# Token transfers over 128 partitions in one DMA, ScalarE copies ahead of some products, and a new order, in an S4 + gated-MLP block

## The chip, the cores and the metric

One core of one Trainium2 chip. The time is device microseconds (us) of one execution, the median over several. With one core a run's state can only be told from other runs of the same kernel: a run over 1.5% above the fastest is called slow.

## The reference, cut to what matters

```python
# L = 2048 tokens, D = 512 channels, F = 1792 hidden, N = 128 modes; bfloat16
x  = A_u                                   # [1, 2048, 512]
xn = layernorm(x)
def _A_ref(u, A, B, C, log_dt, Dskip):     # S4: a long convolution per channel
    K  = einsum("dn,dnl,dn->dl", C, exp(dt * A * l), dt * B).real
    y  = irfft(rfft(pad(u)) * rfft(pad(K)))[:L]
    return y + u * Dskip
def _B_ref(x, w_gate, w_up, w_down):       # gated MLP
    h = sigmoid(x @ w_gate) * (x @ w_up)
    return h @ w_down
return x + _A_ref(xn, ...) + _B_ref(xn, ...)
```

## The kernel before

Every operation is recorded with its engine, its inputs and the buffers that it takes and frees, and then emitted in a fixed list `ORDER`. The engines run their own streams in that order and wait for each other through semaphores. The parts that the change touches:

```python
# token t = (2*a + j)*16 + i sits in partition 64*j + a
xv   = A_u[0].rearrange("(a j i) d -> j a i d", j=2, i=NT)
outv = out[0].rearrange("(a j i) d -> j a i d", j=2, i=NT)

def load_x(i0, n):                         # first token loads: i0 = 0, 2, 4, 8, 12
    ls = [load("ACT" if i0 < 4 and j else "SP", xn[64 * j:64 * j + 64, i0:i0 + n, :],
               xv[j][:, i0:i0 + n, :], 64 * n * KB, pkt=1024 * n, hv=1 - j) for j in range(2)]
# ... (cut)
le = dma("SP", es, cten["E"].ap()[:, gs, :, :], ...)(320 * KB)   # one unit of the spectrum table
# ... (cut)
def final(t, gdeps):                       # output of 2 token rows per partition
    # ... (cut: inverse transform on TensorE, add on VectorE into one of 3 output buffers)
    a = dma("SP", outv[0][:, isl, :], lambda: ot()[0:64], deps=[fin], ...)(128 * KB)
    dma("ACT", outv[1][:, isl, :], lambda: ot()[64:128], deps=[fin, a], rel=[osl], ...)(128 * KB)
# ... (cut)  gated MLP, 4 token groups x 14 units:
mu = pl.add("PE", 0.864, fu, ...)          # up product into a PSUM bank (one of 3)
def fpd(sl=b, h=h):                        # sigmoid(gate) * up, up read from PSUM
    V.tensor_tensor(out=h(), in0=h(), in1=bank(sl), op=ALU.mult)
prods.append(pl.add("DVE", 0.60, fpd, [es_, mu], PPROD, rel=[b]))
# ... (cut)  last group: residual rows of its tokens, 512 KB
lx = [dma("SP", xt[64 * j:64 * j + 64], xv[j][:, i:i + 4, :], ...)(256 * KB) for j in range(2)]
# ... (cut)  other groups: residual added into the MLP's result by the DMA itself
for j in range(2):
    def facc(i=i, j=j, fx=fx):
        P.dma_start(out=fx()[64 * j:64 * j + 64], in_=xv[j][:, i - 1:i + 1, :], accum_op=ALU.add)
final(i // 2, acc)
```

PE is TensorE, DVE VectorE, ACT ScalarE, POOL GpSimd (it issues the accumulating DMAs on a software queue), SP SyncE (it issues most other DMAs). SBUF is the on-chip memory, laid out in 128 partitions; PSUM is the one that TensorE writes its results to, in banks.

## Time and profile before

| | before |
|---|---|
| median of four runs | 275.37 us (274.05 to 276.51) |
| span of the profiled run, granted clock | 276.0 us, 0.965 |
| VectorE busy, TensorE busy | 208.6 us (76%), 229.2 us (83%) |
| last up product (TensorE's) ends | 251.36 us |
| from there to the end | 24.6 us |

The span in 40 slices of 6.9 us (the page's part 2). Each digit is a slice's busy share in tenths; `PEclk` is the clock granted to TensorE, in tenths of full speed; the last row is what the DMA engines moved. VectorE stands at 8 or 9 from slice 4 to slice 20, and nearly so to slice 28, so it bounds that stretch; TensorE follows. The last slices move 134 and 97 GB/s.

```profile
PE   7299997969969899878598878596998689799792
...
DVE  3579899998999999999979997979153222685172
...
PEclk9779999997999999999999999989999979999998
...
GB/s 152 190 297 306 201 307 77 40 57 76 31 190 160 233 160 128 100 183 28 184 185 143 222 159 46 130 153 125 93 221 178 223 199 112 190 187 181 217 134 97
```

The chain of waits that ended last (part 4), shares of the span by engine:

```profile
PE 40%; DVE 29%; DMA 16%; ACT 6%; issue 4%; SPq 2%; DVEq 0%; ACTq 0%
```

VectorE's groups by form: the product (L964 of the kernel file), and a multiply of the same size with both inputs in SBUF. Columns: busy us, mean ns of one | idle time before, with what ended it. Reading one input from PSUM makes the same arithmetic take 682 in place of 421 ns.

```profile
L964 DVE TENSOR_TENSOR hT_sb<-hT_sb,bank 128x512 bf16<-128x512 bf16 x56 | 37.0, 682 | 10.7 <-PE bank L957 6.0 <-ACT hT_sb L951 3.7 <-ACT ln_m_f L467 0.8
...
L680 DVE TENSOR_TENSOR big<-big 128x512 bf16<-128x512 bf16 x8 | 3.4, 421 | 0.0
```

The token transfers among the DMA issues: number, KB of each, median us from issue to landing. `POOLq` rows are the accumulations.

```profile
big<-in_A_u_dram SPq DMA_DIRECT2D x8, 256.0 KB, 7.2
glu_sb<-in_A_u_dram POOLq DMA_DIRECT2D x8, 128.0 KB, 3.9
...
out_dram<-big SPq DMA_DIRECT2D x7, 128.0 KB, 3.0
```

Moments of the timeline (start us, length, engine, what, idle time before in brackets): first tokens in, first gate matmul, first up matmul, first product, first output store, and the last eight that SyncE issues. The whole lead-in to the first product is 29 us.

```profile
4.13 0.69 DVE L499 BATCH_NORM_STATS2 stats<-big 128x6 f32<-128x512 bf16 x1 [4.13 <-DMA big<-in_A_u_dram]
...
15.17 12.71 PE L942 MATMUL bank<-xnT,wg_sb 128*128 128x256 bf16 x64
27.72 4.48 PE L957 MATMUL bank<-xnT,wu_sb 128*128 128x512 bf16 x20
...
28.85 0.69 DVE L964 TENSOR_TENSOR hT_sb<-hT_sb,bank 128x512 bf16<-128x512 bf16 x1 [0.75 <-ACT ln_m_f L467]
...
254.84 0.55 SPq L397 DMA_DIRECT2D out_dram<-big  x1
...
263.01 9.67 SPq L397 DMA_DIRECT2D out_dram<-big  x8
```

### The profile page before, as it was taken

How to read it: one execution, taken by the hardware profiler on the slowest of the kernel's cores; microseconds unless marked ns; L12 is line 12 of the kernel's file. 1: busy time of each engine (PE TensorE's matmuls, PEld its weight loads, DVE VectorE, ACT ScalarE, POOL GpSimd, SP SyncE). 2: the span in 40 equal slices, each digit the busy share in tenths (PEclk: the TensorE clock that was granted, in tenths of full speed). 3: DMA queues.
4: the chain of work that ended last, by engine and by line, in shares of the span. 5: the costliest groups of instructions: out<-in, count | busy, mean ns of one | idle time of the engine just before them, and what ended most of it. 6: DMA issues, size and time to landing. Idle time of an engine off the chain costs nothing.

```text
span 276.0 us, 5805 instructions
## 1 busy us (share of the span) xinstructions
PE 229.2 (83%) x2290; PEld 117.6 (43%) x2290; DVE 208.6 (76%) x407; ACT 162.7 (59%) x249; POOL 20.8 (8%) x43
## 2 busy tenths in 40 slices
PE   7299997969969899878598878596998689799792
PEld 2264433323323544355354445243665345444441
DVE  3579899998999999999979997979153222685172
ACT  2289999998998572558385549341356758531000
POOL 3225000020020002003000000000011200000000
PEclk9779999997999999999999999989999979999998
DMA  5899992122066764451765751454386984665743
GB/s 152 190 297 306 201 307 77 40 57 76 31 190 160 233 160 128 100 183 28 184 185 143 222 159 46 130 153 125 93 221 178 223 199 112 190 187 181 217 134 97
DMA packets 51069, 43.42 MB, mean 157 GB/s; under 512 B 13153, under 2 KB 44258, under 8 KB 51042
## 3 DMA queue, kind: packets, MB, share of 16 engines
q1 hardware_dynamic: 47506, 38.73, 50.1%
q0 software_dynamic: 960, 1.57, 3.9%
q10 hardware_dynamic: 2576, 2.75, 3.5%
q8 instruction: 18, 0.29, 0.5%
q14 instruction: 9, 0.07, 0.1%
HBM read 24.43 MB, written 12.06 MB: 132 GB/s over the span
## 4 chain that ended last, share of the span: by engine, by line
PE 40%; DVE 29%; DMA 16%; ACT 6%; issue 4%; SPq 2%; DVEq 0%; ACTq 0%
PE bank L942 11%; PE bank L957 9%; DMA big<-z_scr 8%; PE bank L982 6%; DVE big L681 5%; DVE big L680 5%; PE pair L744 4%; DVE hT_sb L964 4%; PE pair L835 4%; DVE big L685 4%; DVE big L686 3%; DMA ident<-c_ident 3%; DMA big<-big 2%; DMA big<-v_scr 2%; SPq L397 2%
## 5 line engine op out<-in xcount | busy, mean ns | idle before, releaser
L942 PE MATMUL bank<-xnT,wg_sb 128*128 128x512 bf16 (+1 forms) x236 | 57.4, 382 | 1.4 <-ACT hT_sb L951 1.4
L957 PE MATMUL bank<-xnT,wu_sb 128*128 128x512 bf16 x224 | 55.9, 384 | 2.9 <-ACT hT_sb L951 1.5
L982 PE MATMUL bank<-wd_sb,hT_sb 128*128 128x512 bf16 x224 | 52.2, 387 | 3.3 <-ACT glu_sb L1012 3.3
L964 DVE TENSOR_TENSOR hT_sb<-hT_sb,bank 128x512 bf16<-128x512 bf16 x56 | 37.0, 682 | 10.7 <-PE bank L957 6.0
L951 ACT ACTIVATE hT_sb<-bank 128x512 bf16<-128x512 f32 x56 | 32.3, 599 | 15.1 <-PE bank L942 15.0
L841 DVE TENSOR_TENSOR big<-big 128x2048 bf16<-128x2048 bf16 x16 | 19.6, 1223 | 24.8 <-DMA big<-big 8.2
L680 DVE TENSOR_TENSOR big<-big 128x256 bf16<-128x256 bf16 (+5 forms) x52 | 33.1, 636 | 2.5 <-ACT big L721 1.4
L942 PEld LDWEIGHTS <-wg_sb 128*128 128x128 bf16 x236 | 22.8, 101 | 27.9 <-issue 6.8
L982 PEld LDWEIGHTS <-hT_sb 128*128 128x128 bf16 x224 | 21.7, 99 | 30.4 <-issue 6.9
L681 DVE TENSOR_TENSOR big<-big 128x256 bf16<-128x256 bf16 (+5 forms) x52 | 32.9, 633 | 0.0
L957 PEld LDWEIGHTS <-wu_sb 128*128 128x128 bf16 x224 | 20.5, 98 | 28.5 <-issue 7.7
L822 ACT ACTIVATE big<-pair 128x1024 bf16<-128x1024 f32 x16 | 16.3, 1026 | 11.4 <-PE pair L817 7.3
L685 DVE TENSOR_TENSOR big<-big 128x128 bf16<-128x128 bf16 (+5 forms) x52 | 21.9, 420 | 0.8
L835 PE MATMUL pair<-big 128*128 128x256 bf16 x160 | 20.4, 278 | 2.2 <-ACT big L837 0.7
L862 ACT ACTIVATE big<-pair 128x1024 bf16<-128x1024 f32 x16 | 16.4, 1026 | 9.0 <-PE pair L858 5.2
L686 DVE TENSOR_TENSOR big<-big 128x128 bf16<-128x128 bf16 (+5 forms) x52 | 21.6, 416 | 0.0
L837 ACT ACTIVATE big<-pair 128x1024 bf16<-128x1024 f32 x16 | 16.4, 1027 | 7.8 <-PE pair L835 3.4
L835 PEld LDWEIGHTS <-big 128*128 128x128 bf16 x160 | 15.9, 100 | 8.2 <-issue 3.0
L744 PE MATMUL pair<-big 128*32 128x82 bf16 x512 | 11.5, 257 | 8.2 <-DVE big L685 6.3
L645 ACT ACTIVATE big<-pair 128x1024 bf16<-128x1024 f32 x16 | 16.3, 1019 | 1.7 <-DMA z_scr<-big 1.0
L858 PE MATMUL pair<-big 64*64 64x256 bf16 x384 | 13.7, 272 | 3.1 <-ACT big L822 1.6
L817 PE MATMUL pair<-big,m 64*64 64x256 bf16 x128 | 6.6, 288 | 10.2 <-DMA big<-z_scr 10.2
(84 smaller groups left out, 234.2 us busy)
## 6 DMA issues: line engine op xcount, KB each, us to landing
big<-c_E SPq DMA_DIRECT2D x16, 320.0 KB, 4.2
z_scr<-big SPq DMA_DIRECT2D x16, 256.0 KB, 2.6
big<-z_scr SPq DMA_DIRECT2D x16, 256.0 KB, 4.6
big<-big SPq DMA_DIRECT2D x64, 64.0 KB, 2.9
v_scr<-big SPq DMA_DIRECT2D x16, 256.0 KB, 2.6
big<-v_scr SPq DMA_DIRECT2D x12, 256.0 KB, 4.6
big<-in_A_u_dram SPq DMA_DIRECT2D x8, 256.0 KB, 7.2
wu_sb<-in_B_w_up_dram SPq DMA_DIRECT2D x2, 896.0 KB, 6.1
```

Source lines behind the costliest of these rows:

```text
L680: V.tensor_tensor(out=wide(outp), in0=lov, in1=mre, op=ALU.mult)
L681: V.tensor_tensor(out=wide(tb()), in0=lov, in1=mim, op=ALU.mult)
L685: V.tensor_tensor(out=outp[:, :, :, 0, :], in0=outp[:, :, :, 0, :], in1=tb()[:, :, :, 1, :], op=opr)
L686: V.tensor_tensor(out=outp[:, :, :, 1, :], in0=outp[:, :, :, 1, :], in1=tb()[:, :, :, 0, :], op=opi)
L744: T.matmul(pk[32 * t:32 * t + 32, y % 4, :], G[:, r, :, comp, h], H[:, r, :, comp, h], start=(comp == 0), stop=(comp == 1), tile_position= ...
L835: T.matmul(two(sk)[:, o:o + DW], es()[:, g, kt, :], kT[p][:, kt, :], start=kt in (0, NKT - 1), stop=kt >= NKT - 2)
L841: V.tensor_tensor(out=pp().rearrange("p q h m -> p (q h) m"), in0=xx().rearrange("p q h m -> p (q h) m"), in1=kb()[:, 0:2 * DW].unsqueeze( ...
L942: T.matmul(bank(sl)[:, c0:c1], w[:, kt, k * 128:(k + 1) * 128], xnT[:, grp, kt, c0:c1], start=(kt == 0), stop=(kt == KT - 1))
L951: S.activation(out=hT_sb[:, hs.idx, k % 2, :], in_=bank(sl), func=ACT.Sigmoid)
L957: T.matmul(bank(sl), wu_sb[:, kt, k * 128:(k + 1) * 128], xnT[:, grp, kt, :], start=(kt == 0), stop=(kt == KT - 1))
L964: V.tensor_tensor(out=h(), in0=h(), in1=bank(sl), op=ALU.mult)
L982: T.matmul(bank(po), hT_sb[:, hts[k // 2].idx, k % 2, jj * 128:(jj + 1) * 128], wd_sb[:, k, :], start=(k == 0), stop=k == FT - 1, **kw)
```

## The change

Its intent: fewer DMA issues, by moving all 128 partitions of a token transfer at once; a spectrum unit that lies contiguous in memory; cheaper products, by letting ScalarE copy 27 of the 56 up products out of PSUM as bf16 first (which also frees the PSUM bank earlier); and an order made for this. Costs such as 0.55 in `pl.add` only serve to find an order; the device sees `ORDER` alone.

```diff
-                ... E=f(_build_E(S1, M2)))
+                ... E=f(_build_E(S1, M2).reshape(128, NU // 2, 2, NKT, 128).transpose(1, 0, 2, 3, 4)))
+UEV = (1, 8, 13, 14, 16, 18, 19, 24, 25, 26, 28, 29, ..., 42, 45, 48)      # 27 units
-ORDER = [1, 29, 0, 3, 2, 39, ...]                                          # cut
+ORDER = [1, 43, 0, 3, 4, 12, ...]                                          # cut

 def load_x(i0, n):
-    ls = [load("ACT" if i0 < 4 and j else "SP", xn[64 * j:64 * j + 64, i0:i0 + n, :], xv[j][:, i0:i0 + n, :], 64 * n * KB,
-               pkt=1024 * n, hv=1 - j) for j in range(2)]
+    ls = [load("ACT" if i0 == 2 else "SP", xn[:, i0:i0 + n, :], xv[:, :, i0:i0 + n, :].rearrange("j a i d -> j a (i d)"), 128 * n * KB,
+               pkt=1024 * n)]
...
-            le = dma("SP", es, cten["E"].ap()[:, gs, :, :], deps=w_use[0], ...)(320 * KB)
+            le = dma("SP", es, cten["E"].ap()[u], deps=w_use[0], ...)(320 * KB)
...
-        a = dma("SP", outv[0][:, isl, :], lambda: ot()[0:64], deps=[fin], ...)(128 * KB)
-        dma("ACT", outv[1][:, isl, :], lambda: ot()[64:128], deps=[fin, a], rel=[osl], ...)(128 * KB)
+        dma("SP", outv[:, :, isl, :].rearrange("j a i d -> j a (i d)"), lambda: ot(), deps=[fin], rel=[osl], ...)(256 * KB)
...
-                def fpd(sl=b, h=h):
-                    V.tensor_tensor(out=h(), in0=h(), in1=bank(sl), op=ALU.mult)
-                prods.append(pl.add("DVE", 0.60, fpd, [es_, mu], PPROD, rel=[b]))
+                def feu(sl=b, us=us, on=on):
+                    if on:
+                        S.activation(out=us_sb[:, us.idx, :], in_=bank(sl), func=ACT.Identity)
+                eu = pl.add("ACT", 0.48, feu, [mu], PSIG, acq=[us] if on else [], rel=[b] if on else [], alt=(un, 1))
+                def fpd(sl=b, h=h, us=us, on=on):
+                    V.tensor_tensor(out=h(), in0=h(), in1=us_sb[:, us.idx, :] if on else bank(sl), op=ALU.mult)
+                prods.append(pl.add("DVE", 0.33, fpd, [es_, eu, mu], PPROD, rel=[us] if on else [b], alt=(un, 2)))
...
-                    lx = [dma("SP", xt[64 * j:64 * j + 64], xv[j][:, i:i + 4, :], ...)(256 * KB) for j in range(2)]
+                    lx = [dma("SP", xt, xv[:, :, i:i + 4, :].rearrange("j a i d -> j a (i d)"), ...)(512 * KB)]
...
-                for j in range(2):
-                    ...  P.dma_start(out=fx()[64 * j:64 * j + 64], in_=xv[j][:, i - 1:i + 1, :], accum_op=ALU.add)
+                    ...  P.dma_start(out=fx(), in_=xv[:, :, i - 1:i + 1, :].rearrange("j a i d -> j a (i d)"), accum_op=ALU.add)
```

The stores of the last group are merged in the same way (cut). A merged 256 KB transfer then has, in elements (step, count), the DRAM side `[8192, 2] [16384, 64] [1, 1024]` and the SBUF side `[59392, 128] [1, 1] [1, 1024]`. The 2 at the front of the DRAM side is `j`.

## The prediction

> **What bounds it now.** From about 30 to 165 us VectorE is saturated (97 to 99% busy in the table of windows; 208.6 us in all); TensorE, 83% busy over the span, is the nearest limit afterwards. The chain of waits is mostly TensorE (40%) and VectorE (29%), DMA 16%. The timeline shows a short start: first tokens landing 3.4 us after their issue, first gate matmul at 15.2, first up matmul at 27.7, first product at 28.9 us. The tail is short: 128 KB stores land in a median 2.5 to 3.0 us (page, DMA issues).
>
> **Gains.** 27 of 56 products read a bf16 SBUF copy in place of PSUM: 682 ns now; the 128x512 bf16 SBUF multiplies of line 680 take 421 ns (groups by form). That is 27 x 0.26 = 7 us off VectorE, for 27 x 0.6 = 16 us more on ScalarE, which is 59% busy. Most lie in groups 1 and 2, in or near the VectorE-bound stage: worth about 5 us. Spectrum rows keep their 2,560 bytes (320 KB, 4.2 us to landing): under 1 us. Fewer issues (185 to 179 on SyncE, about 0.6 us each) remove little, since SyncE mostly waits.
>
> **Costs.** A 128-row token transfer has the DRAM side [2][64][row] against [128][row] in SBUF. The Trainium skill, "DMA: Bandwidth & Descriptors", section "Why a DMA increments its semaphore by 16 and not by 1", says a DMA is split over the largest k up to 16 that divides the slowest dimension of both sides. Here that is 2. The trace of before agrees where it can be tested: SyncE's queue shows 3,089 four-byte completion packets, 1 modulo 16, and one transfer has one row; 64-row transfers show 16 each. So token transfers go from 16 DMA engines to 2. A 2,048-byte packet takes 84 ns, so 64 packets per engine take 5.4 us for 256 KB; 512 KB about 10.6 us. Whatever is issued behind them waits for its share on those two engines.
>
> Start: the first two loads share the two engines and land near 13 us in place of 4. The next two (512 KB each) stand in front of the later gate weights, B, and the up weights: gate weights near 40 us, up weights 46 to 49, first product about 50. Both bounding engines fall some 20 to 25 us behind; product saving and slack return part: +15 us at the tail.
>
> Tail: the output is 2 MB, 7 stores of 256 KB and smaller ones, about 44 us on two engines, all behind down projection 13; three output buffers come free only as stores land. Estimated from the last up product to the end: 55 us in place of 25, so +30.
>
> **Sum:** 276 + 15 + 30 = about 320 us; range 288 to 348. Faster by over 2%: 0.13; within 2%: 0.06; slower: 0.81.
>
> **What would show it.** Token loads and output stores landing in 6 to 13 us or more; about 50 GB/s in the last slices; low TensorE digits in slices 3 to 6; first up matmul after 40 us; the chain of waits led at its end by DMA to the output. Product mean about 430 ns in SBUF form, 680 in PSUM form.
>
> **What would make it wrong.** If these transfers use all 16 engines, start and tail are as now or better and the product saving shows: 265 to 272 us. If pieces on the two engines overlap better than 84 ns per packet, the loss halves.

## The result, and the profile after

| | before | after |
|---|---|---|
| median of four runs | 275.37 us (274.05 to 276.51) | 361.66 us (358.76 to 363.83) |
| span of the profiled run, granted clock | 276.0 us, 0.965 | 359.4 us, 0.875 |
| VectorE busy | 208.6 us (76%) | 202.0 us (56%) |
| first product starts | 28.85 us | 50.33 us |
| last up product ends | 251.36 us | 304.62 us |
| from there to the end | 24.6 us | 54.8 us |

The ratio is 1.3129, 95% interval 1.3018 to 1.3241. Ratios here are the mean time of one kernel's fast runs over that of the other's of the same rounds, so not quite the ratio of the medians quoted.

The table already splits the loss of 83.4 us in the span: 53.3 us have gone by the end of the last up product, and 30.1 us are added behind it.

The same rows of part 2, after (slices of 9.0 us). TensorE is idle in slices 1 to 3; new holes stand in slices 16, 29 and 31 to 32; the last four slices move 51, 51, 51 and 38 GB/s.

```profile
PE   0009299589789962788799986895493389685100
...
DVE  0307479399878996099699999602241257141210
...
PEclk9999789969969995889899999999588599968755
...
GB/s 47 124 52 180 101 233 125 101 241 3 49 97 58 191 43 127 76 154 168 157 89 159 187 165 126 126 122 92 254 123 152 87 180 148 227 78 51 51 51 38
```

The granted clock is lower too, 0.875 against 0.965. It is lowest (5 tenths) in slices 16, 29, 32 and the last two, in each of which TensorE is busy for less than half of the time or not at all. Gate and up matmuls take a mean 400 and 408 ns in place of 382 and 384, which I estimate from the two pages at some 10 us for all of them, so a slower clock can stand for little of the 83 us.

The chain that ended last is now short (it could be followed only through the tail), and the largest named part of it is the DMA to the output:

```profile
DMA out_dram<-big 6%; DMA big<-v_scr 2%; DMA v_scr<-big 1%; DVE big L929 1%; SPq L402 1%; DVE big L1011 0%; PE pair L913 0%; PE bank L913 0%; PE bank L915 0%; DVEq L929 0%; DVEq L1011 0%
```

The product by form. The 27 that read a copy take 423 ns and never wait for it; the other 29 take 683 ns as before. This part of the change works.

```profile
L976 DVE TENSOR_TENSOR hT_sb<-hT_sb,bank 128x512 bf16<-128x512 bf16 x29 | 19.4, 683 | 10.5 <-PE bank L961 6.5 <-ACT hT_sb L955 3.9
L976 DVE TENSOR_TENSOR hT_sb<-hT_sb,us_sb 128x512 bf16<-128x512 bf16 x27 | 11.1, 423 | 0.0
```

The DMA issues. For SyncE's and ScalarE's transfers this profile gives no landing times at all; the accumulations land after 17.9 and 15.6 us, where their halves of 128 KB had taken 3.9 and 5.8 us.

```profile
big<-in_A_u_dram SPq DMA_DIRECT2D x4, 512.0 KB
...
out_dram<-big SPq DMA_DIRECT2D x7, 256.0 KB
...
glu_sb<-in_A_u_dram POOLq DMA_DIRECT2D x4, 256.0 KB, 17.9
big<-in_A_u_dram POOLq DMA_DIRECT2D x2, 256.0 KB, 15.6
```

The same moments of the timeline. First tokens come at 12.4 us instead of 4.1. A gate matmul waits 6.95 us for gate weights that stand in the queues behind token loads. SyncE's last eight stores, issued within 9.67 us before, now take 32.94 us.

```profile
12.41 0.69 DVE L504 BATCH_NORM_STATS2 stats<-big 128x6 f32<-128x512 bf16 x1 [12.41 <-DMA big<-in_A_u_dram]
...
33.67 2.78 PE L946 MATMUL bank<-xnT,wg_sb 128*128 128x256 bf16 x24
43.94 0.61 PE L946 MATMUL bank<-xnT,wg_sb 128*128 128x512 bf16 x1 [6.95 <-DMA wg_sb<-in_B_w_gate_dram]
...
49.19 1.03 PE L961 MATMUL bank<-xnT,wu_sb 128*128 128x512 bf16 x4
...
50.33 0.69 DVE L976 TENSOR_TENSOR hT_sb<-hT_sb,bank 128x512 bf16<-128x512 bf16 x1 [1.77 <-PE bank L961]
...
312.96 0.60 SPq L402 DMA_DIRECT2D out_dram<-big  x1
317.49 32.94 SPq L402 DMA_DIRECT2D out_dram<-big  x8
```

The waits of three windows, each line: engine and line, what it waited for, us in total, number, longest. First the waits of 140 to 160 us, around the hole in slice 16, where the second and third accumulation run (their packets fill 124.7 to 151.2 us):

```profile
ACT big L650 <- DMA z_scr<-big: 18.7, 1, 18.7
DVE big L685 <- ACT big L726: 12.9, 1, 12.9
...
PE bank L946 <- DMA xnT<-x_scr: 9.8, 1, 9.8
```

Then 240 to 313 us, with the last three (packets from 242.3 to 284.5 us; the first ran from 89.6 to 102.1):

```profile
DVE big L846 <- DMA big<-big: 25.6, 2, 13.2
...
PE pair L822 <- DMA big<-z_scr: 20.9, 2, 11.3
```

Then the tail, 313 to 360 us: the additions wait for an output buffer, that is, for a store to land.

```profile
DVE big L929 <- DMA out_dram<-big: 14.8, 4, 4.6
...
DVE big L1011 <- DMA out_dram<-big: 3.9, 1, 3.9
```

None of the DMAs named in the first two windows (`z_scr`, `xnT`, `big<-big`) was changed. They are ordinary transfers that suffer from something else.

**How many engines a transfer uses, counted.** The trace of DMA packets has 4-byte packets with which each engine that takes part in a hardware-queue transfer reports its end. The Trainium skill, "DMA: Bandwidth & Descriptors", section "Why a DMA increments its semaphore by 16 and not by 1", says that a transfer is split over the largest k up to 16 that divides the slowest dimension (other than 1) of both sides, and that from SyncE and ScalarE only these k engines report. With the DRAM side starting with 2, k is 2. The counts on SyncE's queue agree exactly with k = 2 for every merged transfer:

```
kernel        token transfers on SyncE's queue      4-byte packets counted
after         14 merged                             2,797
merge_out     9 merged, 5 in pairs (below)          2,947 = 2,797 + 5 x (2x16 - 2)
pairs_all     14 pairs, none merged (below)         3,217 = 2,797 + 14 x (2x16 - 2)
perm16        14 merged, DRAM side [16][8] (below)  2,993 = 2,797 + 14 x (16 - 2)
```

### The profile page after: what moved, and what is told of

Same layout as the page of the kernel before. It is cut to its first block, busy times and chain, and to the rows that moved or that the text cites. A ratio compares the mean times of both kernels' runs of the same rounds, so it can differ in the third digit from the quotient of the medians.

```text
span 359.4 us, 5753 instructions
## 1 busy us (share of the span) xinstructions
PE 236.7 (66%) x2260; PEld 122.6 (34%) x2290; DVE 202.0 (56%) x407; ACT 171.8 (48%) x274; POOL 19.1 (5%) x37
## 5 line engine op out<-in xcount | busy, mean ns | idle before, releaser
L946 PE MATMUL bank<-xnT,wg_sb 128*128 128x512 bf16 (+1 forms) x224 | 59.4, 400 | 18.8 <-DMA xnT<-x_scr 9.8
L961 PE MATMUL bank<-xnT,wu_sb 128*128 128x512 bf16 x215 | 57.9, 408 | 5.9 <-DVE hT_sb L976 5.0
L955 ACT ACTIVATE hT_sb<-bank 128x512 bf16<-128x512 f32 x56 | 32.6, 605 | 7.8 <-PE bank L946 7.7
L961 PEld LDWEIGHTS <-wu_sb 128*128 128x128 bf16 x224 | 22.3, 103 | 34.4 <-issue 10.2
L648 PE MATMUL pair<-big,s 64*128 64x512 bf16 x32 | 6.1, 424 | 30.5 <-DMA s<-c_S 27.7
L976 DVE TENSOR_TENSOR hT_sb<-hT_sb,bank 128x512 bf16<-128x512 bf16 x29 | 19.4, 683 | 10.5 <-PE bank L961 6.5
L504 DVE BATCH_NORM_STATS2 stats<-big 128x6 f32<-128x512 bf16 x16 | 10.8, 677 | 24.7 <-DMA big<-in_A_u_dram 24.7
L840 PE MATMUL pair<-big 128*128 128x256 bf16 x160 | 21.8, 290 | 4.3 <-DMA big<-c_E 4.3
L840 PEld LDWEIGHTS <-big 128*128 128x128 bf16 x160 | 16.3, 104 | 10.7 <-DMA big<-c_E 5.1
```

The source lines that it names most:

```text
L840: T.matmul(two(sk)[:, o:o + DW], es()[:, g, kt, :], kT[p][:, kt, :], start=kt in (0, NKT - 1), stop=kt >= NKT - 2)
L946: T.matmul(bank(sl)[:, c0:c1], w[:, kt, k * 128:(k + 1) * 128], xnT[:, grp, kt, c0:c1], start=(kt == 0), stop=(kt == KT - 1))
L955: S.activation(out=hT_sb[:, hs.idx, k % 2, :], in_=bank(sl), func=ACT.Sigmoid)
L961: T.matmul(bank(sl), wu_sb[:, kt, k * 128:(k + 1) * 128], xnT[:, grp, kt, :], start=(kt == 0), stop=(kt == KT - 1))
L976: V.tensor_tensor(out=h(), in0=h(), in1=us_sb[:, us.idx, :] if on else bank(sl), op=ALU.mult)
```

## The experiments

The theory after the result: the two engines explain the whole loss, and it went past the prediction because the prediction gave the six accumulations no time, though they too were merged. Rivals: the new order itself is bad on the chip; the copies load ScalarE too much; the spectrum's layout costs; the transfers are slow for another reason than the number of engines; the late start grows in the new order, rather than being returned.

Fourteen kernels ran, in four groups, each on one chip with its own runs of the kernel before (medians of all of them 278.72, 278.86, 277.31 and 278.60 us; the last are mostly slow, see there). All but one run that is named gave correct results within the comparison's tolerance. A loss is told against `pairs_all`, the common reference; its own median is 263.86 us.

### All token transfers in pairs again, the rest kept (pairs_all)

```diff
-    ls = [load(..., xn[:, i0:i0 + n, :], xv[:, :, i0:i0 + n, :].rearrange("j a i d -> j a (i d)"), ...)]
+    ls = [load(..., [xn[64 * j:64 * j + 64, i0:i0 + n, :] for j in range(2)], [xv[j][:, i0:i0 + n, :] for j in range(2)], ..., split=True)]
```

The same is done to the late load, the accumulations and the stores; `split` issues the two halves one after the other, in the place of the merged one. Order, copies and spectrum stay as after.

> The changed kernel, its order, copies and spectrum layout kept; every token transfer issued as two 64-row transfers in place of one of 128 rows. Theory A (the whole loss is the two engines): the loss is gone, 255 to 275 us, first up matmul before 35 us, stores landing in under 4 us. Theory B (the new order or the ScalarE copies cost the middle stage): 295 to 320 us, the waits of VectorE on ScalarE in the middle stay.

Measured: **263.86 us** (262.03 to 264.71), ratio to before 0.947 (0.9413 to 0.9527). So the merging costs 97.8 us, and the rest of the change is a gain of 5%. After ran in another group (before 275.37 us there, 278.72 here); if each is scaled by its ratio to its own runs of the kernel before, the merging costs about 102 us. Order, copies and spectrum together are not what lost. The kernel beats both others. Its slices (6.6 us) show no holes, and the tail moves 120 GB/s:

```profile
PE   0499999999999899788999989597969959997692
...
GB/s 144 242 329 291 125 243 232 42 60 70 69 80 216 203 162 228 62 167 179 137 165 99 210 163 148 107 124 83 201 281 203 216 193 212 143 101 267 176 119 120
```

### One kind of token transfer merged at a time (merge_x, merge_acc, merge_out, merge_xt)

Each is `pairs_all` with one kind merged as after: the five first loads, the six accumulations, the output stores, the late residual load. The edits are the corresponding lines of the diff above.

> As pairs_all, but the five first token loads (2 MB) are the merged 128-row ones. If the late start is mostly returned by slack and the saturated stage, as the prediction had it: pairs_all + 10 to 20 us. Theory C (the start's delay of 20 to 25 us is never returned, and the third load of 512 KB adds a second wait): pairs_all + 25 to 45 us.

> As pairs_all, but the six token accumulations (256 KB each, from the software queue) are the merged ones. Theory A with the middle loss put down to them (each lands in 13 to 18 us and holds up the transposes and the spectrum traffic on two engines): pairs_all + 15 to 40 us. Theory C (they are off the critical path): pairs_all + 0 to 6 us.

> As pairs_all, but the output stores are the merged ones. All theories: the tail alone is slow, 44 us of stores at about 50 GB/s from the first store to the end, pairs_all + 22 to 32 us.

> As pairs_all (263.9 us), but the one late residual load of 512 KB is the merged one. It holds two engines for about 10.6 us in front of the spectrum traffic of the second half: pairs_all + 3 to 11 us if that traffic is on the critical path there, + 0 to 2 us if it has slack.

| kernel | merged | median us | ratio to before | loss against pairs_all | of it, gone by the end of the last up product (234.47 in pairs_all) |
|---|---|---|---|---|---|
| merge_x | 5 first loads, 2 MB | 296.35 | 1.0646 | 32.5 | 31.1 |
| merge_acc | 6 accumulations, 1.5 MB | 305.55 | 1.0976 | 41.7 | 40.1 |
| merge_out | stores, 2 MB | 289.75 | 1.0409 | 25.9 | -1.2 |
| merge_xt | 1 late load, 512 KB | 271.87 | 0.9806 | 8.0 | 7.8 |

The losses sum to 108.1 us, where all together cost 97.8 (or about 102, scaled as above): they nearly add, with 6 to 10 us of overlap. Three lie in the ranges expected (`merge_x` in that of theory C), and `merge_acc` is 1.7 us above its own. The last column is read from the timelines of the profiled runs. The costliest kind is the accumulations, which the prediction did not cost.

How an accumulation costs: `merge_acc` against `pairs_all`. The DMA waits of the whole run of `merge_acc`:

```profile
PE pair L824 <- DMA big<-z_scr: 24.0, 3, 12.5
...
ACT big L652 <- DMA z_scr<-big: 22.1, 3, 18.8
DVE big L848 <- DMA big<-big: 18.5, 2, 14.4
...
PE bank L948 <- DMA xnT<-x_scr: 10.0, 1, 10.0
```

and of `pairs_all`, where ScalarE waits 0.3 us in all for `z_scr` and the matmul none for `xnT`:

```profile
PE pair L824 <- DMA big<-z_scr: 8.8, 4, 3.7
...
DVE big L848 <- DMA big<-big: 8.7, 2, 4.6
...
ACT big L652 <- DMA z_scr<-big: 0.3, 1, 0.3
```

So unchanged transfers on SyncE's queue land late. The packet records say why. All 768 accumulating packets carry 2,048 bytes and take a median 176 to 178 ns in before, after, `pairs_all` and `merge_acc` alike; a copied 2,048-byte packet on SyncE's queue takes a median 84 ns in after (101 in before and 126 in `pairs_all`; the lowest quarter ends at 84 ns in all three). Merged, each accumulation is 64 packets on each of two engines, and 64 x 176 ns is 11.3 us. Measured from the first packet to the last: 12.5 us, against 1.2 us for the 64 packets of one half in before. In that time SyncE's queue creeps, in stretches of 3 us (GB/s from packet sizes):

```
merge_acc, from us      90    93    96    99   102   105   108   111   114
accumulations          12.5  17.8  21.9  21.9  15.9  25.5  19.8  19.8  19.1
SyncE's queue          49.2  18.9  23.8  22.0  56.7 242.3  19.1   9.6  36.6
```

A low rate alone could mean that little is asked for; the 10.0 and 18.8 us waits above say that the transfers in these stretches were waited for. In 96 to 102 us all packets of SyncE's queue carry 256 bytes: 279 and 258 of them start in the two stretches, and 32 accumulating ones in each. Spread evenly over 16 engines that is 16 to 17 on each, and the accumulation has 16 on each of its two: one for one, though an accumulating packet carries eight times as much (the trace does not name a packet's engine, so the even spread is assumed). This fits what the Trainium skill says in "DMA: Bandwidth & Descriptors", section "Queues, rings and completion order": each engine takes turns between the queues that have work for it, packet by packet, and one DMA is split over the engines of its queue. A transfer over 16 engines is only complete when its share on the two busy engines is, and the 4-byte packets show that. In `merge_acc` the DMAs to `x_scr` (512 KB) and `z_scr` (256 KB) are issued at 101.4 and 102.0 us. A group of 4-byte packets on SyncE's queue ends at 109.2 us; then come two at 114.8 and two at 118.0, when the accumulation ends as well. From 110 to 118 us 76 packets of the two transfers start, beside 74 accumulating ones. The load of `xnT`, which reads `x_scr`, is issued at 115.2 us, and ScalarE's wait of 18.8 us for `z_scr` ends at 118.7. After shows the same: two late packets at 147.8 and two at 151.3 us, and its wait of 18.7 us ends at 152.0.

The software queue sends 5,376 packets of 8 bytes as well (6 x 14 x 64: each of the 14 idle engines gets as many as a busy one gets packets of data); `pairs_all` sends none.

### Is it the number of engines? (perm16, perm4)

```diff
-    xv = A_u[0].rearrange("(a j i) d -> j a i d", j=2, i=NT)
-    outv = out[0].rearrange("(a j i) d -> j a i d", j=2, i=NT)
+    xv = A_u[0].rearrange("(a j i) d -> j a i d", j=16, i=NT)     # perm16; perm4 has j=4
+    outv = out[0].rearrange("(a j i) d -> j a i d", j=16, i=NT)
```

Nothing but the DRAM side's front changes, from `[2][64]` to `[16][8]` or `[4][32]`: the same bytes, the same merged issues. The tokens then lie in other partitions than the convolution takes them to be in, so these kernels are not right.

> The changed kernel with one number changed: the DRAM side of every token transfer is [16][8][row] in place of [2][64][row]. Same bytes, same row lengths, same count of DMAs; the result is wrong on purpose, since tokens sit on other partitions. If the slowest dimension sets the number of engines: as pairs_all, 258 to 268 us, completion packets 16 a transfer. If merging over 128 rows is slow for another reason (strided rows, one DMA for all partitions): 340 us or more.

> The same with [4][32][row]: four engines, so each token transfer takes about half as long as in the changed kernel (2.7 us of packets for 256 KB in place of 5.4). The loss of 98 us should shrink to about half or less, as waits are hidden first: 285 to 315 us. If engines are not the cause: as the changed kernel.

Measured: `perm16` **260.32 us** (260.02 to 261.75), ratio 0.94 (0.9297 to 0.9502). The whole loss is gone with one number. `perm4` 307.25 us in its fast run (the other, 313.46, was slow), so close to half the loss is left. A whole 256 KB store of `perm16` (first line) lands in 2.9 us, where each half in `pairs_all` takes 2.3 us and one is issued after the other; an accumulation lands in 4.1 us in place of 17.9:

```profile
out_dram<-big SPq DMA_DIRECT2D x7, 256.0 KB, 2.9
glu_sb<-in_A_u_dram POOLq DMA_DIRECT2D x4, 256.0 KB, 4.1
```

The halves in `pairs_all`:

```profile
out_dram<-big SPq DMA_DIRECT2D x14, 128.0 KB, 2.3
```

The 8-byte packets of the software queue are none in `perm16` and 2,304 (6 x 12 x 32) in `perm4`, and its accumulations last 1.8 to 2.4 and 7.0 to 8.2 us where they stand alone: 2, 4 and 16 engines, seen in the packets. Against what I wrote, both were reported correct. Layer norm, MLP and residual work token by token, so a consistent permutation leaves them right, and only the convolution is permuted; that its share is small enough to stay within the tolerance is my inference, and no run shows it. These two are instruments, not kernels to use. Merging at 16 engines is worth 3.5 us over pairs (different groups of runs on one chip).

### Is it the adding, or the width? (merge_acc_plain, merge_acc_early)

```diff
 # merge_acc_plain, against pairs_all (wrong on purpose)
-                        for j in range(2):
-                            P.dma_start(out=fx()[64 * j:64 * j + 64], in_=xv[j][:, i - 1:i + 1, :], accum_op=ALU.add)
+                        P.dma_start(out=fx(), in_=xv[:, :, i - 1:i + 1, :].rearrange("j a i d -> j a (i d)"))
 # merge_acc_early: merged as after for i < 6 (three of six), in pairs for the others
```

> As merge_acc (305.6 us), but the six transfers copy in place of adding; two engines still, and a wrong result on purpose. An adding packet of 2,048 bytes takes 176 ns and a copying one 84. If what hurts is that the packets of other transfers wait turn by turn behind the 176 ns ones on the two engines: the loss of 42 us falls to about half, 278 to 292 us. If the number of engines alone is what hurts, whatever a packet takes: 300 us or more.

> As pairs_all (263.9 us), but only the first three of the six accumulations (those of the first two groups' token pairs, which run before 125 us) are the merged ones. If the loss of 42 us of merge_acc comes from both halves: pairs_all + 12 to 25 us. If only the accumulations near the end matter, where there is the least work to hide them: pairs_all + 0 to 6 us.

Measured: `merge_acc_plain` 274.54 us, ratio 0.994 (0.9813 to 1.0067); its result is wrong (relative error 0.86). The loss falls from 41.7 to 10.7 us, below the expected range (`pairs_espec`, on the same chip as this run and as fast as `pairs_all`, gives 11.0). Its transfers consist of 4,096-byte packets at 159 ns, 32 on each engine, and where they stand alone they hold the two engines for 6.3 to 6.7 us where the adding ones hold them for 12.5. So both are needed for most of the loss: two engines, and packets that take about twice as long for their bytes. The copy also has half as many packets, each nearly as long (159 against 176 ns), so this run does not tell fewer turns from less time. The loss falls by more than the holding time does; a hold of 6 us is partly covered by slack that one of 12 us exceeds, which is argued, not shown.

`merge_acc_early`: 281.6 us in its fast run; the profiled one, 286.56, was slow, so its profile is not used. Three early accumulations cost about 17.7 us by that one run (against `pairs_all` of another chip), leaving some 24 us for the other three. Both halves matter.

### Is the late start returned? (merge_x4, before_merge_x)

```diff
 # merge_x4, against merge_x: the fifth load in pairs
+        if i0 < 12: ...merged...
+        else: ...pairs...
 # before_merge_x, against before: the five first loads merged, nothing else
-        ls = [load("ACT" if i0 < 4 and j else "SP", xn[64 * j:64 * j + 64, i0:i0 + n, :], xv[j][:, i0:i0 + n, :], ...) for j in range(2)]
+        ls = [load("ACT" if i0 < 4 and j else "SP", xn[:, i0:i0 + n, :], xv[:, :, i0:i0 + n, :].rearrange("j a i d -> j a (i d)"), ..., skip=j != (i0 == 2)) for j in range(2)]
```

> As merge_x (296.4 us), but the fifth token load is a pair of 64-row ones again. If its wait of 5.9 us on VectorE adds to the late first product: 288 to 292 us (pairs_all + 24 to 28). If the late first product alone sets the loss: 295 us or more.

> The kernel before and its order, with the first token loads alone merged over 128 rows (two engines). In its order the second and third loads of 512 KB also stand in front of the parameter loads. If a saturated VectorE stage returns nothing whatever the order: before + 20 to 35 us, and the ladder's last step as late as the end. If the old order has slack that the new one lacks: before + 5 to 15 us, as the prediction had it.

Measured: `merge_x4` 286.93 us (286.57 to 289.2), that is 23.1 us over `pairs_all`, a little below what was expected. `before_merge_x` 308.70 us (307.51 to 310.67). On its chip only one of the seven runs of the kernel before counts as fast, 273.40 us; against it the loss is 35.3 us, and against the median of all seven, 278.60, it is 30.1: at the top of the expected 20 to 35, and far from 5 to 15. In `merge_x4` the first up matmul starts at 49.69 us against 23.36 in `pairs_all`, 26.3 us later; the end of the span comes 21.9 us later. So most of a late start stays to the end; 4.4 us are returned. The old order returns no more: in `before_merge_x` the first up matmul starts at 60.21 us against 27.72 in before, 32.5 us later, and the span is 32.6 us longer (308.6 against 276.0, different groups of runs). That the stretch bound by VectorE, which follows, has nothing to give back is the likely reason; no run isolates it. The fifth load adds about 9 us in `merge_x` (296.35 against 286.93, different chips).

### The gain underneath (before_copy, pairs_espec, pairs_16copies)

```diff
 # before_copy, against before: the copy right ahead of the product, in the old order, for the same 27 units
+                    if on:
+                        S.activation(out=us_sb[:, un % 2, :], in_=bank(sl), func=ACT.Identity)
-                    V.tensor_tensor(out=h(), in0=h(), in1=bank(sl), op=ALU.mult)
+                    V.tensor_tensor(out=h(), in0=h(), in1=us_sb[:, un % 2, :] if on else bank(sl), op=ALU.mult)
 # pairs_espec, against pairs_all: the old spectrum layout
-            le = dma("SP", es, cten["E"].ap()[u], ...)
+            le = dma("SP", es, cten["E"].ap()[:, gs, :, :], ...)
 # pairs_16copies, against pairs_all: 11 of the 27 copies undone
-UEV = (1, 8, 13, 14, 16, 18, 19, 24, 25, 26, ..., 42, 45, 48)
+UEV = (1, 8, 13, 14, 16, 24, 26, 31, 32, 33, 35, 36, 38, 40, 45, 48)
```

> The kernel before, with nothing changed but the same 27 up products copied to bf16 SBUF by ScalarE just ahead of their product, in the old order. If the copies are what makes pairs_all 5% faster: 262 to 270 us. If they only pay with the new order: 274 to 282 us; ScalarE work put into a full stage could even cost: up to 284.

> As pairs_all, with the spectrum weights back in the old layout (rows of 2,560 bytes, 20,480 bytes apart, in place of 2,560 apart). The prediction put the new layout at under 1 us: 262 to 266 us. If scattered rows cost DRAM time: 267 us or more, with landings over 4.5 us.

> As pairs_all, with 11 of the 27 copies undone (those without which the same order still builds; the others give a PSUM bank back early, and the order cannot be had without them). VectorE gets 11 x 0.26 = 2.9 us more, ScalarE 11 x 0.6 = 6.6 us less. If VectorE's saving is what the copies are for: 265 to 269 us. If the early release of PSUM banks matters more, or ScalarE is the tighter one: 258 to 265 us.

Measured: `pairs_espec` 263.55 us (263.04 to 265.39), the same as `pairs_all`: the layout is worth nothing here.

`before_copy` 292.57 us, ratio 1.0543 (1.0365 to 1.072): slower, outside all that I expected. The products did become cheap (424 ns), and then waited for their copies:

```profile
L971 DVE TENSOR_TENSOR hT_sb<-hT_sb,us_sb 128x512 bf16<-128x512 bf16 x27 | 11.4, 424 | 27.0 <-ACT us_sb L970 26.9
```

A copy that stands right ahead of its product puts ScalarE's latency in front of a saturated VectorE. In the new order the same 27 products wait 0.0 us.

`pairs_16copies` 269.14 us (268.49 to 270.54): eleven copies fewer cost 5.3 us (different chips), more than the 11 x 0.26 = 2.9 us of VectorE time they save, and just above the range expected if that saving were all. A kernel with this order and no copies could not be had: its PSUM banks would run out, because the order counts on a copy to free its bank early. So how the 5% divides between order and copies stays open.

## Why the prediction was right or wrong

**Right: the mechanism.** k = 2 for the merged transfers, counted in the packets, and shown by `perm16`, where one changed shape removes the whole loss.

**Right: the start.** Loads "near 13 us" came at 12.4; up weights "46 to 49" gave the first up matmul at 49.2; first product "about 50" came at 50.3. Only the gate weights, "near 40", were waited for until 43.9.

**Right: the tail.** "55 us in place of 25, so +30" is 54.8 in place of 24.6, +30.1, with the last slices at 51 GB/s and the waits for output buffers to show it. `merge_out` alone costs 25.9 us. The landing times forecast for the stores could not be checked, since the profile has none.

**Right: the products.** 423 and 683 ns against 430 and 680. The Trainium skill, "VectorE: DVE Perf Modes", section "The perf-mode tier table (the rule you actually need)", has it that an addition or product of two bfloat16 tensors in SBUF runs in a mode twice as fast as one with any operand in PSUM; 423 against 683 ns, fixed cost included, agrees in direction. The spectrum's "under 1 us" is right too.

**Wrong: "product saving and slack return part: +15 us at the tail", the middle term of "276 + 15 + 30".** All that happens up to the last up product was put at +15 us; it measured +53.3. So 38.3 us of the 41.7 by which 361.66 went past the 320 are in this term. What the runs put in its place, in us at the end of the last up product:

```
order, copies and spectrum       -16.9   (pairs_all 234.47 against before 251.36)
five first loads                 +31.1   (merge_x)
six accumulations                +40.1   (merge_acc)
late residual load                +7.8   (merge_xt)
stores                            -1.2   (merge_out)
overlap of these                  -7.6   (the remainder)
                                 +53.3
```

The first two rows alone give +14.2, which is the +15 predicted for start and gains: right only as a sum, and so by luck. The first product did come 21.5 us late, as "20 to 25 us behind" has it, but little was returned and the fifth load added some 9 us, while the gains were larger than thought. The failing is that the sum holds nothing for the accumulations and the late load, 48 us before overlap. The argument had noticed that "whatever is issued behind them waits for its share on those two engines", and applied it to the start only. All that was needed stood in the profile of before: the accumulations among the DMA issues, and their packets' 178 ns. The estimate 64 packets x 178 ns = 11.4 us on each of two engines, or 68 us of two blocked engines for the six, could have been made.

**Half right: TensorE's slices.** The low digits were to be in slices 3 to 6. They are in 1 to 3 and 5, and the holes in 16, 29 and 31 to 32, where accumulations run, were not foreseen.

**Open.** How order and copies share the 5%; why the kinds overlap by 6 to 10 us; how much each accumulation costs by where it stands.

## What to carry to other kernels

Before merging two DMAs, look at the slowest dimension of each side of the merged one: 128 partitions on one side do not help if the other side starts with a 2, and "fewer issues" then buys two engines in place of sixteen. List every transfer that the change touches and give each its own term, accumulations too, and ask of each what else is waiting on the same engines while it runs. Where such a change has several parts, undo the parts one at a time: here the unwanted part hid a version 5% faster than the kernel before.

## What the Trainium skill lacked or had wrong

- "DMA: Bandwidth & Descriptors", section "Rules for kernel authors", says of two transfers to disjoint halves of the partitions that they should be one 128-partition transfer. That is the change studied here. It holds where the merged shape still divides by 16 (`perm16`, 260.32 us, against pairs, 263.86), and costs 97.8 us where the merged DRAM side starts with 2. Another row of that section, "Use all 16 engines", has the condition (a front dimension under 16 confines a DMA to at most that many engines); the row on halves does not say that it applies.
- The same page, section "SDMA does more than copy", gives no rate for accumulating, and I found on no page the time of one accumulating packet; "Collectives: The Full Stack", section "The bandwidth ceiling: the fold count and why AG ≠ RS ≠ AR", has only a collective's adding step, at about half the rate of its copying one. A 2,048-byte accumulating packet took a median 176 to 178 ns here, a copied one 84 ns in after.
- I found on no page what a narrow transfer does to others: while one accumulation ran on two engines, unchanged transfers over 16 fell to 19 to 24 GB/s (93 to 102 us in `merge_acc`), their last two reports came 5.6 and 8.8 us after the others, and single waits of 10.0 and 18.8 us followed.
- The same page says that on the software queue all 16 engines report, whatever the shape. Each accumulation has 16 four-byte packets (96 for six), which agrees; not told is that each idle engine also gets as many 8-byte packets as a busy one gets packets of data (5,376 with 2 engines, 2,304 with 4, none with 16).
- I found on no page that a profile can leave out landing times: after has none for any transfer of SyncE's and ScalarE's queues, only for the accumulations. `merge_out` and `perm4`, whose stores use 2 and 4 engines, have none either; `perm16`, where all use 16, has nearly all.
